# Sink attention into experts on one core: side products issued later, and the first expert's two column blocks interleaved

## The chip, the cores and the metric

One core of a Trainium2 chip. The metric is the device time of one execution of the program in microseconds (us); of three runs the median before is 1338.66 us (1338.24 to 1338.86). TensorE (PE in the profile), VectorE (DVE), ScalarE (ACT), GpSimd (POOL) and the queue on SyncE (SP) each work through their own instructions in program order.

## The reference

```python
# attention: q, k, v of 2 batches x 8 heads x 768 positions x 64
keep = (pos_k < 4) | ((pos_q - pos_k >= 0) & (pos_q - pos_k < 128))
a = softmax(where(keep, q @ k.T / 8, -1e9));  x = a @ v          # -> 1536 x 512
# mixture of 8 experts, D = 512, F = 1024
P = exp(x @ w_gate - max);  8 times: rows to 1, columns to 1, times 1536/8
out = sum_e P[:, e] * (relu(x @ w1[e]) @ w2[e])
# last layer, 512 -> 2048 -> 512
h = out @ w_in;  return (h * cos(h)) @ w_out
```

## The kernel before

All precise products are made from float16 pairs, a high part and a low part, so each matrix product is three products on TensorE. Tensors are scaled by a power of two first. `scales` (L122) finds that factor: VectorE cuts the maxima to powers of two, ScalarE writes them on the diagonals of small matrices (L139), a matmul with ones (`product`, L146) spreads them over all partitions, and VectorE reads the result back (L151). `split` (L173) makes the pair: the high part on ScalarE (or VectorE, where `by` is set), and one step later the low part, usually on VectorE (L183, or L177 without a factor).

**The order is written out by hand.** `put(t0, every, steps)` enters functions into a table of steps, and `run(n)` issues step n: first what was left in the list `late` in the step before, then what the table has for n. A function that appends to `late` thus postpones its work by one step. In the expert part the same is done by `tick`, once after each group of matmuls.

**The attention** works through 48 units (batch b, head pair p, 128 queries i), 24 for each batch. Unit k starts in step 2k (2k+4 in batch 1): `scores` on TensorE (L525) into two banks of the ring "s"; VectorE masks them and takes the maximum (L535); ScalarE exponentiates (L545) and rounds to float16 (`high`, L568) into a buffer of the ring `a16s`; GpSimd makes the low part (L574); SP issues a transposing DMA (`turn`, L584); 13 steps after its scores the unit's products with v follow (`values`, L597 and L602) and VectorE divides by the row sum (`norm`, L614). The ring `a16s` has five buffers, and three from step 58 on; the ring "s" has four banks, and two from step 58 on.

`prep_v` (L433) makes the float16 pair of v for one batch: maxima, one call of `scales` for a group of head pairs (which writes n diagonals into `W1O` and multiplies n times), then for each head pair the split (`sp`) and `sinks` (L463), two matmuls with the matrix `rep` (L466) that copy out the four sink rows, and one VectorE operation (L467). `prep_gate` does it for the gate's weights, `w_load` for an expert's.

`x_operand` (L186) makes the first expert layer's moving operand of 128 tokens from the attention's output: three sums (L197 to L199), high parts on ScalarE, low parts, and a transposing DMA on SP (L205) into `XO`. In batch 0 this happens six times, for c = 0, 1 and i = 0, 1, 2, in steps 37, 41, 45, 53, 57 and 61.

**The first expert layer** replaces a 2 x 2 block product by seven products (numbered o = 0 to 6) of prepared sums of blocks. `w1_split` (L251) makes the sums of the weights on GpSimd (L266 to L269) and their pairs in `W1O`, for one of four column blocks j in four steps. In `g1` (L923) two column blocks, c = 0 and 1, belong to one call, and `chain` names the order of the 14 products (L960, six matmuls each). Products 0, 4, 3 and 6 of a block add up in one bank ("A"), 5 and 2 in another ("B"), 1 has a third ("C"); after 0, 4 and 3 ScalarE copies the sum so far out of "A" (L928), and VectorE adds pairs (L932). `ONE` is the chain of the first expert's first batch, in which the "B" bank of both blocks is the same bank:

```python
ONE = tuple((c, o) for c in range(2) for o in (0, 5, 4, 1, 3, 6, 2))
banks(A0=(2,), A1=(7,), B0=(3,), B1=(3,), C=(6,), g2=(5, 7), l=(5,))
```

Steps up to 69 are issued before the experts. From step 70 on the attention's steps are spread over the ticks of the first expert's first batch: one step per product for 27 ticks, then two steps in three ticks. `g2_mm` (L1028) is the second layer. The weights of the first expert's second layer come through two buffers that they share with the sums of `w1_split`.

Of the kernel before, what the change touches and what calls it, by code (L numbers as in the profile page):

```python
# [40 lines left out]
def kernel(  # L41
# [14 lines left out]
    nc = tc.nc  # L56
# [65 lines left out]
    def scales(parts, n, clamp, keep, tag, then, squares=False, out=None):  # L122
# [34 lines left out]
        late.append(lambda: late.append(product))  # L157
# [8 lines left out]
    late = []  # L166

# [44 lines left out]
    wsc = {}  # L212
# [9 lines left out]
    def w_load(e, nm, place, st, junk=None):  # L222
# [21 lines left out]
        def scl():  # L244
            m = sm.tile([128, 1], F32, tag="wmm", name="wmm")
            nc.vector.tensor_reduce(out=m, in_=st[nm, "m"], axis=AX.X, op=ALU.max)
            scales(m, 1, 1e-30, res, f"{nm}{e}", lambda *s: wsc.update({(e, nm): s}), junk is not None)
# [50 lines left out]
    def attention():  # L298
# [134 lines left out]
        def prep_v(b, groups):  # L433
# [13 lines left out]
            def scl(g, sq):  # L447
                scales(m[:, g], g.stop - g.start, 1e-30, sm, "", lambda *s: None, sq, (sv[:, g], siv_[:, g]))
# [25 lines left out]
            for n, g in enumerate(groups):  # L474
# [5 lines left out]
                for p in range(g.start, g.stop):  # L480
                    steps.append(lambda p=p: sp(p))
                    steps.append(lambda p=p: sinks(p))
# [4 lines left out]
        def prep_gate():  # L487
            wgm = sm.tile([128, 1], F32, tag="wgm", name="wgm")
            absmax(wgm, wgf.rearrange("p k e -> p (k e)"))

            def then(s, si):
                split(wg[:, 0], wg[:, 1], wgf, s)
                swg.append(si)

            scales(wgm, 1, 1e-30, res, "wg", then)
# [195 lines left out]
        def ops(b, c, i, s0):  # L691
            box = []
            put(s0, 1, [lambda: box.append(x_operand(
                b, c, i, None, *(() if b else ((Ts, xss), *((nc.gpsimd, nc.vector)[n] for n in ((0, 0), (1, 0))[c])))))])
            put(s0 + 2, 1, [lambda: box.pop()()])
# [26 lines left out]
        put(15, 2.5, p0[10:-1:2])  # L722
        put(26, 1, [prep_gate])
        put(12, 1.5, wl1[4:])
        put(28, 2.75, w1_split(0, st, range(1)))
        put(14, 2.0, [lambda p=p: load_v(1, p) for p in range(NP)])
        p1 = prep_v(1, (slice(0, NP),))
        put(24, 2.5, p1[-1:] + p1[:5] + [lambda: None] + p1[5:-1])

        def run(n):  # L730
            flush()
# [4 lines left out]
        for n in range(-2, start):  # L736
            if n == ends[0] - 8:

                banks(s=(0, 1), x=(4,))
                a16s.parts[3:] = []  # L740
# [4 lines left out]
                w1_split(0, st, range(1, NJ)))  # L745
# [49 lines left out]
    def experts(before):  # L795
# [124 lines left out]
        ONE = tuple((c, o) for c in range(2) for o in (0, 5, 4, 1, 3, 6, 2))  # L920
# [224 lines left out]
        put(0, 1, w1_rest[:4])  # L1145
        put(4, 1, w1_rest[4:8])
        put(9, 1, w1_rest[8:])
# [108 lines left out]
```

## Time and profile before

| | |
|---|---|
| median of three runs | 1338.66 us |
| the profiled execution: own time | 1336.99 us |
| its span, first to last instruction | 1335.2 us |
| busy: PE / DVE / ACT / POOL | 1266.1 / 837.5 / 708.1 / 653.9 us |
| TensorE's clock, mean granted share | 0.976 |

A row of a timeline gives the start (us from the span's start), the duration, engine, line, operation, output and inputs, and in brackets how long the engine had been idle before it and what ended the wait. A row of the waits gives the waiting instruction, whom it waited for, total us, how often, and the longest. L numbers are lines of the kernel.

### The profile page before, as it was taken

The numbers are of one execution on the slowest core, as the hardware profiler recorded it, in microseconds if no ns is written. First come the engines' busy times: TensorE is split into PE (matmuls) and PEld (weight loads), VectorE is DVE, ScalarE is ACT, GpSimd is POOL, SyncE is SP. The second block draws the span as 40 slices with busy tenths as digits, with TensorE's granted clock in tenths as the row PEclk, the third lists the DMA queues.
The fourth block names the chain that finished last, engine by engine and source line by source line (L and its number), as shares of the span: only waits on it lengthen the run. The fifth ranks groups of instructions, "written<-read, shape, count | busy, mean of one in ns | idle before, by whom it ended". The sixth has DMA issues, their size and how long they took to land.

```text
span 1335.2 us, 19606 instructions
## 1 busy us (share of the span) xinstructions
PE 1266.1 (95%) x7269; PEld 676.5 (51%) x7269; DVE 837.5 (63%) x1608; ACT 708.1 (53%) x1493; POOL 653.9 (49%) x817
## 2 busy tenths in 40 slices
PE   5657899999999999999999999999999998999998
PEld 4544546555554545555454555545455544445454
DVE  6676624765548555853755575375556688788674
ACT  7866836373633537163353716335372757566452
POOL 5766664340633454272335427233541857376543
PEclk7868999999999999999999999999999998999999
DMA  9988661021013210501321150132102241400001
GB/s 259 172 172 169 139 116 58 9 107 64 13 64 111 95 64 32 174 0 64 112 94 63 32 174 1 63 112 94 64 32 83 52 105 28 105 1 1 32 17 48
DMA packets 135472, 106.67 MB, mean 80 GB/s; under 512 B 98000, under 2 KB 110288, under 8 KB 135376
## 3 DMA queue, kind: packets, MB, share of 16 engines
q1 hardware_dynamic: 121296, 75.12, 21.7%
q0 software_dynamic: 7168, 25.17, 6.0%
q10 hardware_dynamic: 6912, 5.13, 1.3%
q8 instruction: 57, 0.93, 0.3%
q14 instruction: 39, 0.32, 0.1%
HBM read 70.27 MB, written 11.53 MB: 61 GB/s over the span
## 4 chain that ended last, share of the span: by engine, by line
PE 71%; DVE 5%; POOL 4%; ACT 3%; issue 3%; DMA 1%; POOLq 0%; DVEq 0%; ACTq 0%
PE bank L1028 38%; PE bank L960 28%; PE bank L977 4%; DVE tmp L991 2%; DVE tmp L897 1%; DMA xo<-xs 1%; POOL hh L877 1%; DVE tmp L888 1%; ACT xs L182 1%; DVE xs L183 1%; ACT tmp L885 0%; ACT tmp L893 0%; POOL S L268 0%; DVE w1o L183 0%; POOL S L269 0%
## 5 line engine op out<-in xcount | busy, mean ns | idle before, releaser
L1028 PE MATMUL bank<-w2s,hh 128*128 128x512 f16 x2880 | 637.0, 379 | 2.6 <-POOL hh L901 2.1
L960 PE MATMUL bank<-xo,w1o 128*128 128x384 f16 x2688 | 448.9, 327 | 11.3 <-ACT acc L928 7.4
L1028 PEld LDWEIGHTS <-hh 128*128 128x128 f16 x2880 | 281.2, 98 | 334.7 <-POOL hh L901 4.8
L877 POOL TENSOR_TENSOR hh<-tmp,hh 128x384 f16<-128x384 f32 x240 | 217.6, 927 | 352.7 <-ACT tmp L876 350.8
L960 PEld LDWEIGHTS <-w1o 128*128 128x128 f16 x2688 | 260.9, 98 | 185.9 <-issue 16.9
L928 ACT ACTIVATE tmp<-bank 128x384 f32<-128x384 f32 x180 | 87.5, 487 | 300.0 <-PE bank L960 299.9
L932 DVE TENSOR_TENSOR tmp<-bank,tmp 128x384 f32<-128x384 f32 x180 | 97.6, 554 | 175.9 <-ACT tmp L928 130.8
L977 PE MATMUL bank<-xo,w1o 128*128 128x384 f16 x672 | 120.4, 329 | 6.5 <-ACT tmp L999 3.6
L1097 DVE SCALAR_TENSOR_TENSOR acc<-bank,PS,acc 128x512 f32<-128x512 f32 x84 | 62.9, 748 | 81.6 <-PE bank L1028 81.2
L876 ACT ACTIVATE tmp<-tmp 128x384 f32<-128x384 f32 x180 | 94.2, 523 | 5.7
L977 PEld LDWEIGHTS <-w1o 128*128 128x128 f16 x672 | 66.0, 99 | 58.0 <-issue 10.9
L875 ACT ACTIVATE hh<-tmp 128x384 f16<-128x384 f32 x180 | 92.6, 515 | 1.8 <-DVE tmp L932 1.7
L899 POOL TENSOR_SCALAR hh<-tmp 128x384 f16<-128x384 f32 x64 | 45.7, 715 | 82.7 <-DVE tmp L897 72.9
L182 ACT ACTIVATE w1o<-S,s 128x1024 f16<-128x1024 f32 x40 | 45.8, 1145 | 74.4 <-POOL S L269 74.4
L160 DVE TENSOR_REDUCE wm<-st 128x1 f32<-128x1024 f32 x68 | 81.5, 1208 | 0.0
L183 DVE SCALAR_TENSOR_TENSOR w1o<-st,s,w1o 128x512 f16<-128x512 f32 x72 | 65.1, 935 | 14.0 <-ACT w1o L182 13.9
L183 DVE SCALAR_TENSOR_TENSOR w1o<-S,s,w1o 128x1024 f16<-128x1024 f32 x40 | 55.2, 1381 | 26.6 <-ACT w1o L182 26.6
L901 POOL TENSOR_TENSOR hh<-tmp,hh 128x384 f16<-128x384 f32 x64 | 68.8, 1076 | 5.3
L183 DVE SCALAR_TENSOR_TENSOR w2s<-st,s,w2s 128x512 f16<-128x512 f32 x72 | 60.2, 848 | 17.5 <-ACT w2s L182 17.4
L991 DVE TENSOR_TENSOR tmp<-bank,tmp 128x384 f32<-128x384 f32 x112 | 59.1, 548 | 10.9 <-PE bank L977 6.7
L574 POOL TENSOR_TENSOR parts<-xo,parts 128x512 f16<-128x512 f32 (+1 forms) x38 | 42.8, 1125 | 24.5 <-ACT parts L568 18.3
L893 ACT ACTIVATE tmp<-tmp,scl 128x384 f32<-128x384 f32 x64 | 39.1, 610 | 26.9 <-DVE tmp L888 26.9
(187 smaller groups left out, 1308.2 us busy)
## 6 DMA issues: line engine op xcount, KB each, us to landing
st<-in_moe_w_dram SPq DMA_DIRECT2D x56, 512.0 KB, 6.0
f<-in_moe_w_in_dram POOLq DMA_DIRECT2D x16, 512.0 KB, 4.4
f<-in_moe_w_out_dram POOLq DMA_DIRECT2D x16, 512.0 KB, 4.2
w2p<-in_moe_w_dram SPq DMA_DIRECT2D x8, 512.0 KB, 4.3
w_in<-x POOLq DMA_DIRECT2D x16, 256.0 KB, 4.4
w_out<-x POOLq DMA_DIRECT2D x16, 256.0 KB, 4.2
st<-w_out SPq DMA_DIRECT2D x8, 512.0 KB, 5.4
st<-w_in SPq DMA_DIRECT2D x8, 512.0 KB, 6.5
```

What stands on the lines that cost most here:

```text
L160: nc.vector.tensor_reduce(out=dst, in_=src, axis=axis, op=ALU.max, apply_absolute_value=True)
L183: late.append(lambda: nc.vector.scalar_tensor_tensor(out=lo, in0=src, scalar=s, in1=hi, op0=ALU.mult, op1=ALU.subtract))
L875: nc.scalar.activation(out=hi, in_=src, func=AF.Relu)
L876: nc.scalar.activation(out=dst, in_=src, func=AF.Relu)
L877: nc.gpsimd.tensor_tensor(out=lo, in0=dst, in1=hi, op=ALU.subtract)
L901: nc.gpsimd.tensor_tensor(out=lo, in0=k, in1=hi, op=ALU.subtract)
L928: nc.scalar.activation(out=t, in_=ps, func=AF.Copy)
L932: nc.vector.tensor_tensor(out=t, in0=ps, in1=t, op=ALU.add)
L960: nc.tensor.matmul(ps, W1O[:, j0 + c, wi, o, kk, :], XO[b][:, kk, o, xi, :], start=(n == 0 and o in (0, 5, 1)), stop=(n == 5), skip_group_ ...
L977: nc.tensor.matmul(ps, W1O[:, j, wi, o, kk, :], XO[b][:, kk, o, xi, :], start=(n == 0), stop=(n == 5))
L991: nc.vector.tensor_tensor(out=t, in0=x, in1=y, op=ALU.add)
L1028: nc.tensor.matmul(ps, HH[:, hi, f, t * 128:(t + 1) * 128], w[:, wi, f, :], start=(f == order[0] and n == 0), stop=(f == order[-1] and n = ...
```

## The change

- `scales` gets the argument `lag`, the number of steps from the diagonals to the matmul: 2 as before, 3 for the second group of batch 0, 5 for the group of batch 1, the gate and the first expert's first weights. `later(n, f)` puts f off by n steps.
- The sink rows of batch 0 (head pairs 1 to 3) move from steps 15, 17 and 20 to 19, 24 and 29; those of batch 1 are issued six steps after their place in the list. The list of batch 1 is spaced by two steps, not two and a half, with two empty entries more.
- The last operand block of batch 0 (c = 1, i = 2) makes the pair of its sums one step sooner, with the low part on VectorE, not GpSimd; its DMA follows one step sooner.
- The sums and pairs of column block j = 1 are made in steps 58 to 62, not in ticks 0 to 4; those of j = 2 and 3 in ticks 2 to 5 and 7 to 10, not 4 to 7 and 9 to 12.
- The ring `a16s` keeps five buffers up to step 77.
- `ONE` alternates between the blocks c = 0 and c = 1.

```diff
--- before.py
+++ after.py
@@ -119,7 +119,7 @@
     diag = res.tile([128, 128], BF16, name="diag")
     top_bank = ["l"]
-    def scales(parts, n, clamp, keep, tag, then, squares=False, out=None):
+    def scales(parts, n, clamp, keep, tag, then, squares=False, out=None, lag=2):
@@ -154,7 +154,7 @@
             then(s, si)
-        late.append(lambda: late.append(product))
+        later(lag, product)
     def absmax(dst, src, axis=AX.X):
         nc.vector.tensor_reduce(out=dst, in_=src, axis=axis, op=ALU.max, apply_absolute_value=True)
@@ -164,6 +164,9 @@
     BW = ((1, 1, 0), (0, 1, 0), (1, 0, 0), (0, 1, 0))
     late = []
+
+    def later(n, f):
+        late.append(f if n <= 1 else lambda: later(n - 1, f))
     def flush():
         now, late[:] = late[:], []
@@ -244,7 +247,8 @@
         def scl():
             m = sm.tile([128, 1], F32, tag="wmm", name="wmm")
             nc.vector.tensor_reduce(out=m, in_=st[nm, "m"], axis=AX.X, op=ALU.max)
-            scales(m, 1, 1e-30, res, f"{nm}{e}", lambda *s: wsc.update({(e, nm): s}), junk is not None)
+            scales(m, 1, 1e-30, res, f"{nm}{e}", lambda *s: wsc.update({(e, nm): s}), junk is not None,
+                   lag=5 if e == 0 else 2)
         return [lambda i=i: load(i) for i in range(4)] + [lambda i=i: amax(i) for i in range(4)] + [scl]
@@ -445,7 +449,8 @@
                     absmax(m[:, p:p + 1], vt[:, p].rearrange("p t c -> p (t c)"))
             def scl(g, sq):
-                scales(m[:, g], g.stop - g.start, 1e-30, sm, "", lambda *s: None, sq, (sv[:, g], siv_[:, g]))
+                scales(m[:, g], g.stop - g.start, 1e-30, sm, "", lambda *s: None, sq, (sv[:, g], siv_[:, g]),
+                       5 if b else 3 if g.start else 2)
             def common():
@@ -479,7 +484,7 @@
                     steps.append(common)
                 for p in range(g.start, g.stop):
                     steps.append(lambda p=p: sp(p))
-                    steps.append(lambda p=p: sinks(p))
+                    steps.append(lambda p=p: later(6, lambda: sinks(p)) if b else sinks(p))
             return steps + [ones_col]
         swg = []
@@ -492,7 +497,7 @@
                 split(wg[:, 0], wg[:, 1], wgf, s)
                 swg.append(si)
-            scales(wgm, 1, 1e-30, res, "wg", then)
+            scales(wgm, 1, 1e-30, res, "wg", then, lag=5)
@@ -690,9 +695,11 @@
         def ops(b, c, i, s0):
             box = []
+            last = not b and c and i == U3 - 1
             put(s0, 1, [lambda: box.append(x_operand(
-                b, c, i, None, *(() if b else ((Ts, xss), *((nc.gpsimd, nc.vector)[n] for n in ((0, 0), (1, 0))[c])))))])
-            put(s0 + 2, 1, [lambda: box.pop()()])
+                b, c, i, None, *(() if b else (
+                    (Ts, xss), *((nc.gpsimd, nc.vector)[n] for n in ((0, 0), (1, int(last)))[c])))))])
+            put(s0 + (1 if last else 2), 1, [lambda: box.pop()()])
         ends = []
         for b in range(B):
@@ -719,15 +726,18 @@
         put(6, 1.0, p0[4:7])
         put(9, 4, p0[7:9])
         put(13, 0.5, p0[9:-1:2])
-        put(15, 2.5, p0[10:-1:2])
+        put(19, 5, p0[10:-1:2])
         put(26, 1, [prep_gate])
         put(12, 1.5, wl1[4:])
         put(28, 2.75, w1_split(0, st, range(1)))
+        put(ends[0] - 8, 1.25, w1_split(0, st, range(1, 2)))
         put(14, 2.0, [lambda p=p: load_v(1, p) for p in range(NP)])
         p1 = prep_v(1, (slice(0, NP),))
-        put(24, 2.5, p1[-1:] + p1[:5] + [lambda: None] + p1[5:-1])
+        put(24, 2.0, p1[-1:] + p1[:5] + [lambda: None] * 3 + p1[5:-1])
         def run(n):
+            if n == start + 8:
+                a16s.parts[3:] = []
             flush()
             for f in at.pop(n, ()):
                 f()
@@ -737,12 +747,11 @@
             if n == ends[0] - 8:
                 banks(s=(0, 1), x=(4,))
-                a16s.parts[3:] = []
             run(n)
         gates = [[lambda b=b, i=i: gate(b, i) for i in range(NT)] for b in range(B)]
         return ([lambda n=n: run(n) for n in range(start, ends[1])], gates, probabilities,
-                w1_split(0, st, range(1, NJ)))
+                w1_split(0, st, range(2, NJ)))
     def sinkhorn():
@@ -917,7 +926,8 @@
         CHAIN = ((0, 0), (1, 0), (0, 5), (0, 4), (1, 4), (1, 5), (0, 3), (1, 3), (0, 1), (0, 6), (1, 6),
                  (0, 2), (1, 2), (1, 1))
-        ONE = tuple((c, o) for c in range(2) for o in (0, 5, 4, 1, 3, 6, 2))
+        ONE = ((0, 0), (0, 5), (1, 0), (0, 4), (0, 1), (0, 3), (1, 4), (0, 2), (0, 6), (1, 5), (1, 3), (1, 1),
+               (1, 6), (1, 2))
         HOME = {0: "A", 4: "A", 3: "A", 6: "A", 5: "B", 2: "B", 1: "C"}
         def g1(b, j0, chain, act):
@@ -1142,9 +1152,8 @@
             put(1, 1, [f()])
         put(5, 4, [lambda f=f: gate(f) for f in gates[0]])
-        put(0, 1, w1_rest[:4])
-        put(4, 1, w1_rest[4:8])
-        put(9, 1, w1_rest[8:])
+        put(2, 1, w1_rest[:4])
+        put(7, 1, w1_rest[4:])
         a = ACC[0].rearrange("p t c -> p (t c)")
         ring["c"] = Ring(a[:, n * HT:(n + 1) * HT] for n in range(8))
         put(T0 + 0, 2, [lambda f=f: gate(f) for f in gates[1]])
```

## Rows read from the trace of the kernel before

**Rows 1.** Six stretches: us, length, busy us (instructions) by engine, granted clock, DMA.

```profile
0.00:62.00 62.00, 38.37 (x301) 29.14 (x302) 41.16 (x154) 47.62 (x135) 39.22 (x89) 0.83 1.00 221
62.00:100.00 38.00, 22.30 (x187) 15.18 (x187) 26.55 (x91) 23.88 (x68) 24.92 (x33) 0.66 0.88 169
100.00:140.00 40.00, 29.79 (x270) 17.13 (x267) 27.29 (x67) 26.88 (x66) 26.30 (x32) 0.90 0.75 156
140.00:164.20 24.20, 21.63 (x245) 13.16 (x244) 14.55 (x47) 22.48 (x57) 15.72 (x20) 1.00 0.70 156
164.20:178.70 14.50, 12.05 (x123) 6.61 (x120) 6.46 (x19) 8.05 (x21) 10.40 (x17) 1.00 0.53 101
178.70:1335.20 1156.50, 1141.92 (x6163) 595.28 (x6158) 721.47 (x1233) 579.17 (x1149) 537.37 (x629) 1.00 0.21 65
```

**Rows 2.** Waits of PE, 0 to 62 us: total us, times, longest.

```profile
PE bank L146 <- ACT w1o L139: 6.8, 2, 3.5
...
PE bank L597 <- DVE hh L467: 3.0, 2, 2.6
PE bank L146 <- ACT diag L139: 2.4, 2, 2.3
```

**Rows 3.** Waits of ACT, 9 to 62 us.

```profile
ACT nm L538 <- DVE mx L535: 4.0, 4, 1.5
```

**Rows 4.** Waits of PE, 62 to 100 us.

```profile
PE bank L525 <- DVE mx L535: 4.6, 4, 1.9
...
PE bank L466 <- DVE w2s L183: 3.4, 3, 1.6
PE bank L466 <- ACT w2s L182: 2.4, 3, 1.3
```

**Rows 5.** One stretch; columns: PE, PEld, DVE, ACT, POOL, clock, DMA.

```profile
74.90:86.70 11.80, 8.52 (x75) 5.70 (x75) 10.39 (x37) 5.75 (x18) 4.97 (x8) 0.61 0.88 191
```

**Rows 6.** Same stretch, tile w1o (PE, PEld, DVE, ACT), then S (DVE, ACT, POOL).

```profile
106.50:114.70 8.20, 3.42 (x18) 1.60 (x18) 4.09 (x4) 1.84 (x2) 1.00 0.55 120
...
106.50:114.70 8.20, 1.27 (x1) 1.14 (x1) 3.29 (x4) 1.00 0.55 120
```

**Rows 7.** Timeline of DVE, low parts of two operand blocks.

```profile
85.41 0.62 DVE L177 TENSOR_TENSOR w2s<-acc,w2s 128x256 f16<-128x256 f32 x2
...
92.27 1.57 DVE L177 TENSOR_TENSOR w2s<-acc,w2s 128x256 f16<-128x256 f32 x2
```

**Rows 8.** Timeline of POOL at 92 to 97 us.

```profile
92.36 1.33 POOL L574 TENSOR_TENSOR parts<-xo,parts 128x512 f16<-128x512 f32 x1 [1.52 <-ACT parts L568]
...
95.37 1.16 POOL L177 TENSOR_TENSOR w2s<-hh,w2s 128x512 f16<-128x512 f32 x1 [1.47 <-ACT w2s L176]
```

**Rows 9.** Timeline of SP's queue at 96 to 105 us.

```profile
96.56 2.11 SPq L205 DMA_TRANSPOSE xo<-w2s  x1
98.77 5.76 SPq L584 DMA_TRANSPOSE parts<-parts  x3
```

**Rows 10.** Timeline of ACT at 98 to 104 us.

```profile
103.78 0.42 ACT L568 ACTIVATE parts<-xo 128x256 f16<-128x256 f32 x1 [5.25 <-DMA parts<-parts]
```

**Rows 11.** Timeline of PE, three places in the first expert.

```profile
102.83 0.65 PE L960 MATMUL bank<-xo,w1o 128*128 128x384 f16 x3 [1.68 <-DMA xo<-w2s]
...
116.00 2.08 PE L960 MATMUL bank<-xo,w1o 128*128 128x384 f16 x6 [3.85 <-ACT acc L928]
...
123.20 1.15 PE L960 MATMUL bank<-xo,w1o 128*128 128x384 f16 x6
```

**Rows 12.** One stretch of 3 us, all engines.

```profile
116.00:119.00 3.00, 3.00 (x19) 1.46 (x19) 2.90 (x7) 2.39 (x7) 2.92 (x5) 0.50 0.91 192
```

**Rows 13.** Waits of PE, 100 to 164 us.

```profile
PE bank L960 <- ACT acc L928: 7.4, 6, 3.9
...
PE bank L960 <- DVE acc L932: 1.6, 1, 1.6
PE bank L146 <- ACT diag L139: 1.2, 1, 1.2
```

## The prediction

> **What bounds the kernel now.** I read the busy time by stage first, then each engine's waits in the stages where TensorE is not full, then the timelines around the longest waits. From 178.7 us on TensorE is busy for 1141.92 of 1156.5 us [rows 1]; nothing of the change is issued there, so all of its effect lies in the first 178.7 us. Those are four stages. From 0 to 62 us (the attention's first batch) ScalarE is the fullest engine, 47.62 of 62 us. From 62 to 100 us (the second batch up to the first expert) no engine is full on average. From 100 to 164.2 us the first expert's first layer and the second batch share all engines: TensorE is idle for 40.0 - 29.79 = 10.2 us in the first 40 and for 24.2 - 21.63 = 2.6 us in the rest, where ScalarE works for 22.48 of 24.2 us, 93%. The last 14.5 us are nearly all TensorE [rows 1].
>
> **The change part by part.** The profiled execution took 1336.99 us for a span of 1335.2, so 1.8 us lie around the span, and it stands 1.7 us under the median of 1338.66. I work out the difference on the span and apply it to the median.
>
> *Later products, 0 to 62 us.* TensorE stood 6.8 us before the matmuls of the two grouped `scales` calls, 2.4 us before those of single ones, and 3.0 us before values products held up by the sink rows' VectorE operation [rows 2]. One of the two grouped waits stays: for batch 0 the lag goes from two steps to three, from step 11 to step 12, ahead of the scores of that step, and TensorE is given nothing between the two, so its place in the queue is the same. The others go. But TensorE is not what this stage waits for. ScalarE does the same work as before, and of its waits only those for VectorE's maxima, 4.0 us in all [rows 3], can be later scores in disguise. That is the ceiling; the floor is nothing (the maxima are late because of VectorE's own queue, which holds the low parts of v). I see late scores behind about half: gain **2.0** (0 to 4.0).
>
> *Sink rows of batch 1, and the work that moves in, 62 to 102.8 us.* TensorE's waits before the sink products are 3.4 + 2.4 = 5.8 us [rows 4]. They vanish when the products come six steps later, behind the splits that they read. Most of that was hidden: VectorE is busy for 10.39 of 11.8 us between 74.9 and 86.7 us [rows 5], and the scores after it wait for VectorE to free banks (4.6 us [rows 4]). I count 0.7 us as a gain, for the one place where the first scores of batch 1 stood behind sink products. Against it, four steps for block j = 1 move into steps 58 to 62. Their price is in the trace, where they now run: 4.09 us on VectorE in four operations, 1.84 us on ScalarE in two, and 3.29 us on GpSimd in four [rows 6]. The last operand block's low part also goes to VectorE. A 512-wide one does not occur there in the rows; two shorter ones took 0.62 us at 85.41 and 1.57 us at 92.27 [rows 7]. I take the lower, as the GpSimd operation that ran beside the slow pair [rows 8] need not be there, and keep 1.57 for the range. So VectorE gets 4.7 us more, in front of scores that have two banks only. Some falls into VectorE's own idle time: 38.0 - 26.55 = 11.5 us in the stage [rows 1], of which half lies after step 58. Three quarters of the 4.7 hidden leaves 1.2 us. GpSimd's 3.29 us come in front of low parts that SP's transposes wait for; GpSimd is idle for 38.0 - 24.92 = 13.1 us, so I cost it at 0.5, and at 3.3 if that cover is gone.
>
> The operand comes sooner: SP began the last operand's DMA at 96.56 us, when GpSimd's 1.16 us at 95.37 were done, and spent 2.11 us on it; three transposes stood behind it until 104.5 [rows 8, 9]; the first product went on at 102.83 after waiting 1.68 us for that DMA [rows 11]. One step sooner, it goes ahead of one more transpose, and a low part late on VectorE would hold that one up. The sooner step undoes part of the shift. Sum for this stage: +1.2 + 0.5 - 0.7 = a loss of **1.0** (a gain of 2 if all is hidden and the 1.7 us wait goes; a loss of 4.7 if nothing of VectorE's work is hidden).
>
> In a sentence of its own: the Trainium skill ("SBUF — State Buffer", section "SBUF: two separate sides") says that GpSimd and a VectorE operation with two SBUF inputs exclude each other on a shared port, one standing still until the other is done, which speaks against putting GpSimd's sums and VectorE's low parts into the same steps. The pairs of 0.62 and 1.57 us agree with it; by the rule each of the three low parts of j = 1 could take 0.95 us more, and this stage would lose 3.9, not 1.0.
>
> *Buffers kept longer, and the first expert, 100 to 164.2 us.* ScalarE stood for 5.25 us up to 103.78 because its next `high` needed a buffer that the queued transposes still read [rows 10]. Two more buffers let it run on; the copy that the third product waits for then comes in time. TensorE's waits here are 7.4 us for ScalarE's copies out of bank "A" (six times), 1.6 for VectorE on the shared bank "B", and 1.2 for the diagonal of the second weights [rows 13], which keeps its lag of two. The new chain leaves one to three products of the other block between a product in "A" and the next in that bank; in the old one product 6 followed 3 at once. So I let the 7.4 go. The "B" pairs have one product between them as before, and the shared bank is handed over as often: 0.8 of 1.6 goes. Of the rest of TensorE's 12.8 us of idle time, 1.7 is the DMA counted above and I take nothing.
>
> There is a second gain. After 3.85 us idle the six matmuls at 116.00 took 2.08 us, where six take 1.15 at 123.20 [rows 11]; the granted clock from 116 to 119 was 0.50 [rows 12], the lower of the two levels, 1.2 GHz. Without the wait that product is 0.9 us shorter. The Trainium skill ("TensorE: Matmul & The Clock Gate", Part 1) has the throttled state as what idling returns the array to; the row agrees.
>
> Together 7.4 + 0.8 + 0.9 = 9.1 us. Part comes back. From 140 us ScalarE is 93% busy and nothing is taken off it there, so at most 1.7 us of that stretch can go, and elsewhere ScalarE and VectorE must now do the same copies and sums in less time. Block j = 1 no longer costs 1.84 us on ScalarE and 4.09 on VectorE here, which helps. I take three quarters: gain **7.0** (2, if each removed wait is replaced by the "B" wait; 11.1, if all idle time but the DMA's goes). The transfers of the second weights are spaced in ticks and have shorter ticks; their buffers change hands with the sums for j = 2 and 3, which move by the same two ticks; I cost that at nothing, and at 1.5 us, one tick at the stage's pace, if a transfer comes late.
>
> *164.2 us to the end.* The same instructions in the same order: 0 (-1 to +1).
>
> Sum: -2.0 + 1.0 - 7.0 = -8.0 us. Span 1327.2, own time 1329.0, median **1330.7**.
>
> **The rivals.**
> *TensorE becomes the bound.* All its idle time in the first expert goes but the 1.2 for the diagonal and the 1.7 for the DMA: 12.8 - 2.9 = 9.9, with 0.9 for the clock 10.8; the first stage gives 3.0 and the second loses nothing: -13.8, 1324.9. For it: each of the three other engines works under 69% of 100 to 140 us [rows 1]. Against: all are in order, and each product's result passes ScalarE, VectorE, ScalarE and GpSimd.
> *The waits were cover.* ScalarE and VectorE set the pace everywhere; TensorE waits elsewhere instead. First stage 0, second +1.5, third -2.5 (clock and half of the longest wait): -1.0, 1337.7. For it: ScalarE's 77% in the first stage and 93% at the end. Against: 5.25 us of ScalarE's idle time [rows 10] is bought off by buffers, not by order.
> *The moved split delays the start.* The low parts of j = 1 stand in VectorE's queue ahead of the maxima, each waiting for ScalarE's high part, while scores have two banks. The 4.7 us are bare, and two waits like the one before the last sink low part (longest 1.6 [rows 4]) add 3.2: +7.9 by the first product, which starts near 109 us; the first expert gives back 5: +2.9, 1341.6. It decides from a first product later than about 107.
>
> **How the numbers follow.** The forecast (1326 to 1336) has 0.54, TensorE as the bound 0.18, waits as cover 0.17, the delayed start 0.11. 0.2% is 2.7 us and about what a measurement can tell from no change; so faster means under 1336.0: 0.54 + 0.18 = 0.72. Same is the third case, 0.17, and slower 0.11. The range goes from 1323.5, which leaves out the further half of the second case, to 1340, which leaves out most of the last. The bounds of the terms sum to 1320.5 (-4.0 - 2.0 - 11.1 - 1.0) and 1342.4 (0 + 4.7 - 2.0 + 1.0).
>
> **What would show it.** TensorE's waits for diagonals and sink splits should be gone but for one of about 3 us near 18 us. ScalarE should have no wait of several us before L568. The first product should start between 100 and 104 us, and TensorE's idle time from there to the second layer should be near 5 us, not 12.8, with the granted clock at 1 throughout. The second layer should begin near 158 us instead of 164.2. I am wrong if the first product starts after 107, or if the wait for L928 reappears as a wait for L932 of like size.

## The result: slower by 0.67%, all of it before the first expert's first product

The median went from 1338.22 us (six runs of the kernel before beside it) to 1346.94 us; the ratio is 1.0067, with a 95% interval of 1.0057 to 1.0077, so about 9 us were lost. Forecast were 1330.7 us, with 1323.5 to 1340.0 as the range. The profiled execution after took 1346.12 us for a span of 1344.4, 9.2 us above the span before.

Six stretches of the changed kernel, in the columns of [rows 1] (us, length, busy us of PE, PEld, DVE, ACT, POOL, clock, DMA). The second one now ends with the first product, the fourth with the second layer:

```profile
0.00:62.00 62.00, 38.12 (x302) 28.83 (x303) 40.64 (x150) 47.37 (x133) 38.28 (x89) 0.86 0.99 221
62.00:112.70 50.70, 23.11 (x186) 15.54 (x185) 34.57 (x99) 28.33 (x79) 30.09 (x39) 0.55 0.82 146
112.70:152.70 40.00, 34.88 (x325) 20.27 (x323) 28.06 (x75) 28.79 (x74) 26.14 (x34) 0.88 0.76 162
152.70:172.30 19.60, 17.64 (x195) 10.74 (x192) 11.77 (x37) 15.76 (x39) 9.61 (x13) 1.00 0.55 131
172.30:188.20 15.90, 12.21 (x124) 6.69 (x121) 6.14 (x17) 9.33 (x25) 11.79 (x18) 1.00 0.49 94
188.20:1344.40 1156.20, 1140.86 (x6158) 594.71 (x6156) 721.76 (x1233) 579.15 (x1149) 537.52 (x629) 1.00 0.21 65
```

The second one before, up to where the first product went on:

```profile
62.00:102.80 40.80, 23.44 (x189) 15.46 (x189) 27.52 (x94) 23.88 (x68) 24.92 (x33) 0.67 0.91 176
```

The last stretch takes 1156.2 us as against 1156.5. The loss is the second: TensorE is busy for 23.11 us in it, much as before, but takes 50.7 us over that and not 40.8, at a mean clock of 0.55. VectorE's busy time rose from 27.52 to 34.57 us.

TensorE's waits, 0 to 62 us, to set beside [rows 2]:

```profile
PE bank L530 <- DVE mx L540: 7.7, 5, 3.3
...
PE bank L146 <- ACT w1o L139: 3.2, 1, 3.2
```

The waits for diagonals and sink rows are gone but for one of 3.2 us (and 0.4 us for a sink split), as forecast. In their place stand 7.7 us before the scores (L530; L525 before) for VectorE's maxima. The first scores of batch 1 begin at 75.92 us, not 76.21. Whether the stage gave anything at all can't be told from that: of kernels whose steps are the same up to there, `before` has 76.21, `buffers_only` 77.21 and `split_alone` 78.96 in their one profile each. All later stretches are therefore counted from these scores.

TensorE's waits from the first product to the second layer, to set beside [rows 13]:

```profile
PE bank L970 <- DVE acc L942: 2.8, 3, 1.0
PE bank L530 <- DVE mx L540: 2.4, 2, 2.2
PE bank L970 <- ACT acc L938: 1.1, 2, 0.9
```

The waits for ScalarE's copies, 7.4 us before, became 1.1, as the interleaved chain should bring. But the stretch shrank only from 61.4 to 59.6 us.

Three places in TensorE's timeline (start, duration, engine, line, operation, xcount, idle time before):

```profile
111.87 0.40 PE L602 MATMUL bank<-w2s,parts 128*128 128x130 f16 x2 [5.80 <-DMA parts<-parts]
...
112.74 2.11 PE L970 MATMUL bank<-xo,w1o 128*128 128x384 f16 x6
...
178.11 0.34 PE L607 MATMUL bank<-w2s,parts 128*128 128x65 f16 x6 [3.01 <-DVE acc L619]
```

The first product, 99.99 us before (and again after its DMA at 102.83 [rows 11]), starts at 112.74. It is not its own operand that is late (sent at 100.76 us, landed at 105.3): ahead of it in TensorE's queue stands a values product that waited 5.80 us for a transposing DMA. The first product runs at the lower clock, 2.11 us for six matmuls where 1.15 is the time at the higher one [rows 11]. The 0.9 us that I had thought to save at 116.00 [rows 11] did not come: over the whole first layer the mean granted clock is 0.92, where it was 0.94 before.

### The profile page after: what moved, and what is told of

Its sections match the earlier page's. It is cut to its first block, busy times and chain, and to the rows that moved or that the text cites. A ratio compares the mean times of both kernels' runs of the same rounds, so it can differ in the third digit from the quotient of the medians.

```text
span 1344.4 us, 19614 instructions
## 1 busy us (share of the span) xinstructions
PE 1266.8 (94%) x7269; PEld 676.8 (50%) x7269; DVE 843.0 (63%) x1609; ACT 708.7 (53%) x1493; POOL 653.4 (49%) x816
## 4 chain that ended last, share of the span: by engine, by line
PE 70%; DVE 5%; POOL 4%; ACT 3%; issue 3%; DMA 1%; POOLq 0%; DVEq 0%; ACTq 0%
PE bank L1038 38%; PE bank L970 28%; PE bank L987 4%; DVE tmp L1001 2%; DVE tmp L906 1%; DMA xo<-xs 1%; POOL hh L886 1%; DVE tmp L897 1%; ACT xs L185 1%; DVE xs L186 0%; ACT tmp L894 0%; ACT tmp L902 0%; POOL S L272 0%; POOL S L273 0%; POOL hh L910 0%
## 5 line engine op out<-in xcount | busy, mean ns | idle before, releaser
L987 PEld LDWEIGHTS <-w1o 128*128 128x128 f16 x672 | 65.9, 98 | 57.6 <-issue 10.2
L186 DVE SCALAR_TENSOR_TENSOR w1o<-st,s,w1o 128x512 f16<-128x512 f32 x72 | 64.7, 930 | 14.0 <-ACT w1o L185 13.9
L186 DVE SCALAR_TENSOR_TENSOR w2s<-st,s,w2s 128x512 f16<-128x512 f32 x72 | 60.2, 848 | 17.5 <-ACT w2s L185 17.4
L186 DVE SCALAR_TENSOR_TENSOR w1o<-S,s,w1o 128x1024 f16<-128x1024 f32 x40 | 54.6, 1365 | 23.2 <-ACT w1o L185 23.2
L579 POOL TENSOR_TENSOR parts<-xo,parts 128x512 f16<-128x512 f32 (+1 forms) x34 | 38.9, 1145 | 31.2 <-ACT parts L573 16.8
```

Of the source, the lines that this page charges most:

```text
L186: late.append(lambda: nc.vector.scalar_tensor_tensor(out=lo, in0=src, scalar=s, in1=hi, op0=ALU.mult, op1=ALU.subtract))
L987: nc.tensor.matmul(ps, W1O[:, j, wi, o, kk, :], XO[b][:, kk, o, xi, :], start=(n == 0), stop=(n == 5))
```

## The experiments

In short, three parts of the change delay the first product. The later products put a split of v in front of the first maxima (2.6 us, won back elsewhere). The moved split fills VectorE's queue, and its sums on GpSimd lengthen VectorE's other operations (3.9 us). The sooner operand holds up a transpose, which then lands late (4.2 us). What the interleaved chain wins in waits it loses again.

All ratios are to the kernel before, run beside it on the same chip; the difference of two ratios is uncertain by about 0.14%, or 1.9 us. Times of stretches come from one profile each: **M** from the first scores of batch 1 to VectorE's first maximum of them; **Q** from there to the first product (to its restart, where it waits for its operand's DMA); **F** from there to the second layer; **T** from there to the end of the last values products. Between kernels that differ elsewhere only, M agrees within 0.4 us (3.6 to 4.0), T within 0.1, Q and F within about 1. Where the first product has a restart, about half of its six matmuls lie before it and count to Q; the changed kernel, `split_undone` and `last_sooner_gpsimd` have none. The letters of the theories in the expectations have nothing to do with the letters of the stretches.

| kernel | ratio, 95% interval | M | Q | F | T |
|---|---|---|---|---|---|
| before | 1 | 1.25 | 25.4 | 61.4 | 14.6 |
| after | 1.0067 (1.0057 to 1.0077) | 3.9 | 33.0 | 59.6 | 15.9 |
| last_undone | 1.0038 (1.0024 to 1.0052) | 3.7 | 28.7 | 59.9 | 17.0 |
| split_undone | 1.0026 (1.0017 to 1.0036) | 3.8 | 26.9 | 62.5 | 14.6 |
| both_undone | 0.9989 (0.9980 to 0.9999) | 3.8 | 24.8 | 59.8 | 14.6 |
| last_sooner_gpsimd | 1.0003 (0.9993 to 1.0013) | 3.6 | 25.6 | 61.0 | 14.6 |
| last_on_vector | 0.9984 (0.9975 to 0.9994) | 4.0 | 24.1 | 58.9 | 14.6 |
| best_again (the same kernel) | 0.9994 (0.9985 to 1.0003) | 3.7 | 24.0 | 59.3 | 14.6 |
| split_alone | 1.0025 (1.0016 to 1.0034) | 1.25 | 29.2 | 59.0 | 17.0 |
| early_split_new_chain | 1.0036 (1.0025 to 1.0048) | 8.1 | 24.1 | 58.8 | 17.0 |
| early_split_old_chain | 1.0020 (1.0011 to 1.0030) | 8.1 | 24.3 | 58.3 | 14.6 |
| sums_on_vector | 1.0025 (1.0016 to 1.0035) | 8.4 | 24.6 | 60.1 | 14.6 |
| vector_load | 1.0001 (0.9990 to 1.0011) | 3.7 | 26.2 | 58.9 | 14.6 |
| gpsimd_load | 1.0014 (1.0005 to 1.0024) | 3.8 | 27.1 | 58.9 | 14.6 |
| lags_only | 1.0008 (0.9997 to 1.0019) | 3.8 | 26.3 | 59.9 | 14.6 |
| buffers_only | 0.9992 (0.9982 to 1.0001) | 1.25 | 26.4 | 58.9 | 14.6 |
| w2_vector_old | 0.9999 (0.9990 to 1.0009) | 4.0 | 24.3 | 60.8 | 14.7 |
| w2_vector_new | 1.0019 (1.0010 to 1.0028) | 8.2 | 24.7 | 59.7 | 14.6 |

### Undoing the two suspects

`last_undone` takes back the operand block, `split_undone` the moved split and the chain, `both_undone` both, so that the later products and the five buffers stay. `split_alone` has nothing but the split and the chain on top of the kernel before.

```diff
# last_undone
-            last = not b and c and i == U3 - 1
+            last = False
# split_undone
-        put(ends[0] - 8, 1.25, w1_split(0, st, range(1, 2)))
-                w1_split(0, st, range(2, NJ)))
+                w1_split(0, st, range(1, NJ)))
-        put(2, 1, w1_rest[:4])
-        put(7, 1, w1_rest[4:])
+        put(0, 1, w1_rest[:4])
+        put(4, 1, w1_rest[4:8])
+        put(9, 1, w1_rest[8:])
-        ONE = ((0, 0), (0, 5), (1, 0), ...)
+        ONE = tuple((c, o) for c in range(2) for o in (0, 5, 4, 1, 3, 6, 2))
```

> The changed kernel with the last operand block as before: low part of its sums on GpSimd, one step later. Theory Q (SP's queue: the DMA of the last operand, now ahead of more transposes and waiting for a low part late on VectorE, holds up the transposes behind it, and TensorE waits 5.8 us for them at 111.87): most of the loss comes back, time 1339 to 1341, first product of the first expert near 106 us, no wait over 2 us before values products there. Theory V (VectorE: the low parts of block j = 1 in steps 58 to 62 stand ahead of the maxima, scores with two banks come 6.9 us later): only the 1.6 us of that low part come back, 1344 to 1346, first product at 110 or later.

> The changed kernel with the old order of the chain ONE and with the sums and pairs of blocks j = 1, 2, 3 in ticks 0, 4 and 9 as before; the last operand block stays sooner and on VectorE. Theory V: the maxima come in time, first product near 102 us, and the first expert loses its interleaving, 1336 to 1339. Theory Q: the DMA of the last operand still stands ahead of the transposes, so TensorE still waits 3 to 6 us before values products near step 67, 1341 to 1345.

> The changed kernel with the last operand block, the chain ONE and the times of the splits as before; later products, later sink rows and five buffers stay. Both theories: the loss is gone. If the later products are worth the 2.0 us that I gave them and the buffers take away the wait of ScalarE at 103.78 (5.25 us): 1331 to 1336. If these waits were cover only: 1337 to 1339.

> The kernel before with the interleaved chain ONE and the block j = 1 made in steps 58 to 62, nothing else. Theory V: the maxima of steps 59 to 65 come 5 to 7 us later and the interleaved chain gives back 2 to 5, so 1340 to 1345. Theory Q: without the sooner operand the queue on SP is not held up, so 1334 to 1339.

Measured: 1.0038, 1.0026, 0.9989 and, for `split_alone`, 1.0025. With both undone the loss is gone. Each theory was half right: the time of `last_undone` (1344.47 us) is what V expects, that of `split_undone` (1342.68 us) what Q expects. From `both_undone`, split and chain cost 0.49% (6.6 us), the operand block 0.37% (5.0 us); together they cost 0.78%, a little less than the sum. The table says where. From `both_undone` to `last_undone` Q grows by 3.9 us, and T by 2.4; from there to the changed kernel Q grows by another 4.2. With M, where the later products add 2.6 and Q gives back 0.5, that is 2.6 - 0.5 + 3.9 + 4.2 = 10.2 us, all of the added time between the first scores of batch 1 and the first product. `split_alone` agrees: without the later products M is 1.25, and Q is 3.8 above the kernel before.

### The operand block: which half of the edit

`last_sooner_gpsimd` makes it one step sooner with the low part still on GpSimd, `last_on_vector` puts the low part on VectorE in the old step; both have split and chain undone, as `both_undone` has. The lines are against `split_undone`:

```diff
# last_sooner_gpsimd
-   (nc.gpsimd, nc.vector)[n] for n in ((0, 0), (1, int(last)))[c]
+   (nc.gpsimd, nc.vector)[n] for n in ((0, 0), (1, 0))[c]
# last_on_vector
-            put(s0 + (1 if last else 2), 1, [lambda: box.pop()()])
+            put(s0 + 2, 1, [lambda: box.pop()()])
```

> As both_undone (1337.9), but the last operand block one step sooner, its low part still on GpSimd. Theory Q: its DMA now stands ahead of one more transpose that is ready, and waits for a low part made no sooner than before: values products wait 4 to 6 us, 1341 to 1344. If it were only the work on VectorE: 1337 to 1339.

> As both_undone (1337.9), but the last operand block's low part on VectorE, in its old step. Theory Q: the order on SP is the old one, so no more than the 0.7 to 1.6 us of that operation, 1337 to 1340. If VectorE's load is the cause of the 4.8 us between split_undone and both_undone: 1341 to 1343.

Measured 1.0003 and 0.9984: the sooner step costs about 0.14%, which is as much as the uncertainty and less than theory Q expected (1340.07 us, not 1341 to 1344), though its values product waited as Q had it, for 5.73 us. VectorE alone costs nothing. The low part of 128x512 took 1.64 us on VectorE in the changed kernel (timeline below), a little over my upper bound of 1.57. Both halves in one cost 0.37%. SP's queue shows how. First `both_undone`, then `split_undone`, which differ by this edit alone (L208 is the operand's DMA, L589 the transposes):

```profile
93.07 3.27 SPq L589 DMA_TRANSPOSE parts<-parts  x2
97.70 3.44 SPq L208 DMA_TRANSPOSE xo<-w2s  x1
```

```profile
95.03 1.81 SPq L589 DMA_TRANSPOSE parts<-parts  x1
97.57 1.51 SPq L208 DMA_TRANSPOSE xo<-w2s  x1
99.18 5.45 SPq L589 DMA_TRANSPOSE parts<-parts  x2
```

TensorE in `split_undone`:

```profile
108.31 0.40 PE L602 MATMUL bank<-w2s,parts 128*128 128x130 f16 x2 [5.43 <-DMA parts<-parts]
```

The operand's DMA has overtaken one transpose. Counted from VectorE's first maximum (80.35 and 82.32 us) it leaves 2.1 us sooner, and the second transpose of the pair at 93.07 now goes behind it, first in the issue at 99.18. In `both_undone` the values product ahead of the first product starts at 100.26 without a wait for a transpose; in `split_undone` it waits 5.43 us. What was gained for the operand is lost on the product ahead of it in TensorE's queue. That is 2.0 us in Q and, as only `both_undone` has a restart, part of the 2.7 in F.

The later issue alone does not make that wait. The DMA view of the issue gives the time from issue to landing (the last number, in us); the transpose in `both_undone`, and then in `split_undone`, where the loads of k and q for the next head pair are under way with it:

```profile
parts<-parts SPq DMA_TRANSPOSE x1, 3.3
```

```profile
xo<-in_k_dram ACTq DMA_DIRECT2D x1, 384.0 KB, 5.1
xo<-in_q_dram ACTq DMA_DIRECT2D x1, 384.0 KB, 8.2
parts<-parts SPq DMA_TRANSPOSE x1, 9.1
```

Sent at 99.18 and landed after 3.3 us, it would have been there at 102.5, before TensorE stood idle at 102.9. It is the 9.1 us that TensorE waits for. In all 18 profiles the first transposing DMA that SP sends from 0.6 us before the k load on takes 6.0 to 9.5 us to land, those that it sends from 88 us up to then 2.9 to 4.6. With the old block that first one is the operand's DMA; in the changed kernel and in `split_undone` it is the transpose for which the values product ahead of the first product waits. In `last_sooner_gpsimd` both were hit, 7.8 us for the operand and 8.0 for the transpose right behind it.

### The moved split: place, and the chain by itself

`early_split_new_chain` makes the sums and pairs of j = 1 twelve steps sooner (46 to 50), before the first scores of batch 1, with the last block undone; `early_split_old_chain` has the old `ONE` besides.

```diff
-        put(ends[0] - 8, 1.25, w1_split(0, st, range(1, 2)))
+        put(46, 1.25, w1_split(0, st, range(1, 2)))
```

> The changed kernel with the last operand block as before and the sums and pairs of block j = 1 in steps 46 to 50, where no scores are issued, not 58 to 62. Theory V: the maxima of steps 59 to 65 no longer stand behind them, first product near 104 us, 1335 to 1339. If the loss of last_undone (1344.5) comes from the interleaved chain or from the total work, not its place: 1342 to 1345.

> As early_split_new_chain with the old chain ONE. My forecast had the new chain worth about 6 us of TensorE's waits, so this would be 1340 to 1345. If ScalarE sets the pace from step 70 to the end of the attention and TensorE's waits were its cover, the two chains differ by less than 2 us.

Measured 1.0036 and 1.0020. The place hardly matters (1.0036 against 1.0038; theory V had the loss gone), so the idea that the split costs only because of where it stands falls. The split costs some 0.31% (from 0.9989 to 1.0020), and the chain is no gain but a loss of 0.16%, just over the uncertainty. TensorE's waits from the first product to the second layer, new chain and then old:

```profile
PE bank L970 <- DVE acc L942: 2.8, 3, 1.0
PE bank L530 <- DVE mx L540: 2.5, 2, 2.2
...
PE bank L970 <- ACT acc L938: 0.6, 2, 0.4
```

```profile
PE bank L969 <- ACT acc L937: 6.2, 5, 2.9
...
PE bank L969 <- DVE acc L941: 1.1, 1, 1.1
PE bank L530 <- DVE mx L540: 0.8, 1, 0.8
```

And the whole stretch, new and then old (columns as in [rows 1]):

```profile
108.07:166.90 58.83, 52.32 (x507) 31.14 (x507) 37.62 (x108) 43.95 (x110) 34.76 (x45) 0.91 0.71 158
```

```profile
110.76:169.07 58.31, 50.20 (x507) 30.20 (x507) 36.33 (x106) 45.05 (x113) 36.40 (x46) 0.94 0.71 160
```

Of 6.2 us of waits for ScalarE 5.6 went; 3.4 came back as waits for VectorE (1.7 each for its sums and its maxima), and the same 507 matmuls took 2.1 us longer, at a mean clock of 0.91 instead of 0.94. The clock is from one profile each. What paces the first layer then is not shown: ScalarE is busy for 75 and 77% of it.

### Is it VectorE's queue or GpSimd's?

From `both_undone`: `vector_load` adds four reductions of 128x1024 (1.21 us each) to VectorE in steps 59 to 62, `gpsimd_load` makes the four sums of j = 1 once more on GpSimd in step 58. Their results are used by nobody, or are the same.

```diff
# vector_load
+        waste = sm.tile([128, 4], F32, tag="waste", name="waste")
+        put(59, 1, [lambda n=n: absmax(waste[:, n:n + 1], st["w1"][:, n, 0:1024]) for n in range(4)])
# gpsimd_load
+        put(58, 1, w1_split(0, st, range(1, 2))[:1])
# sums_on_vector (early_split_old_chain and this)
-                g = nc.gpsimd
+                g = nc.vector if e == 0 and j == 1 else nc.gpsimd
```

> As both_undone (ratio 0.9989, about 1338), with four more VectorE reductions of 1024 elements (1.2 us each, 4.8 in all, result unused) in steps 59 to 62, nothing else. Theory W (VectorE's work is the path of the second batch, so what is added there is added to the first product): 4 to 5 us, 1342 to 1343. If the split's loss came by ScalarE or GpSimd, or by the waits between engines: 0 to 2 us.

> As both_undone, with the four GpSimd sums of block j = 1 (3.3 us) made once more in step 58, their result unused. Theory W: 0 to 1.5 us, what they hold up on the shared port and in front of the transposes, 1337 to 1339.5. If GpSimd's low parts ahead of the transposes are the path: 2 to 4 us, 1340 to 1342.

> early_split_old_chain with one change: the four sums of block j = 1 are made on VectorE instead of GpSimd. Before kernel about 1339; early_split_old_chain was 1342.6 (ratio 1.0020). Theory G (the moved split costs by GpSimd's 3.3 us of sums, which also hold up VectorE's two-input operations): 2 to 3.5 us come back, ratio 0.9995 to 1.0005, 1338.5 to 1340, first scores of batch 1 to the first product's restart about 30 us instead of 32.3. Theory V (it costs by VectorE's queue, which now gets some 1.7 us more): the same or slower, ratio 1.0020 to 1.0035, 1342 to 1344.

Measured 1.0001, 1.0014 and 1.0025: against 0.9989, VectorE's 4.8 us cost 0.12% (1.6 us), within the uncertainty, and GpSimd's 3.3 us of sums 0.25% (3.3 us, give or take 1.9). Both speak against theory W, which had 4 to 5 us for the first and at most 1.5 for the second. Taking the sums off GpSimd, though, bought nothing: theory G, that GpSimd's sums carry the split's price, fails as I had put it. The windows join the two. Here is the stretch in which VectorE makes the maxima of the first seven units of batch 1, for `both_undone`, `gpsimd_load`, `vector_load`, `last_undone` and the changed kernel, one after the other (the third busy time is VectorE's):

```profile
80.35:96.86 16.51, 10.77 (x74) 6.95 (x74) 14.82 (x54) 11.40 (x33) 7.75 (x10) 0.50 0.75 141
```

```profile
80.97:99.51 18.54, 11.19 (x74) 7.29 (x74) 17.19 (x54) 11.32 (x33) 11.55 (x14) 0.50 0.66 127
```

```profile
81.02:100.21 19.19, 10.13 (x74) 6.61 (x74) 17.84 (x58) 11.42 (x33) 7.39 (x10) 0.59 0.70 133
```

```profile
82.31:103.58 21.27, 11.19 (x74) 7.29 (x74) 18.49 (x58) 13.06 (x36) 12.22 (x14) 0.50 0.61 116
```

```profile
79.79:102.61 22.82, 11.19 (x74) 7.28 (x74) 19.86 (x59) 13.58 (x38) 12.66 (x14) 0.50 0.56 107
```

VectorE is busy for 87 to 93% in all of them, more than any other engine: it is the bound here. GpSimd's sums bring no instruction to it (54 in both), yet add 2.4 us to its busy time. Its timeline in the changed kernel and GpSimd's beside it show how:

```profile
87.74 0.70 DVE L202 TENSOR_TENSOR hh<-acc,hh 128x128 f32<-128x128 f32 x1
88.36 2.10 DVE L180 TENSOR_TENSOR w2s<-acc,w2s 128x256 f16<-128x256 f32 x2
...
92.56 1.13 DVE L186 SCALAR_TENSOR_TENSOR w1o<-tmp,s,w1o 128x512 f16<-128x512 f32 x1 [1.06 <-ACT w1o L185]
...
96.77 0.29 DVE L202 TENSOR_TENSOR hh<-acc,hh 128x128 f32<-128x128 f32 x1
96.97 0.62 DVE L180 TENSOR_TENSOR w2s<-acc,w2s 128x256 f16<-128x256 f32 x2
...
97.88 1.28 DVE L186 SCALAR_TENSOR_TENSOR w1o<-S,s,w1o 128x1024 f16<-128x1024 f32 x1 [0.29 <-ACT w1o L185]
99.09 1.64 DVE L180 TENSOR_TENSOR w2s<-hh,w2s 128x512 f16<-128x512 f32 x1
```

```profile
85.08 1.44 POOL L270 TENSOR_TENSOR S<-tmp 128x256 f32<-128x256 f32 x1
...
87.52 0.78 POOL L272 TENSOR_TENSOR S<-tmp 128x256 f32<-128x256 f32 x1
88.25 0.77 POOL L273 TENSOR_TENSOR S<-tmp,S 128x256 f32<-128x256 f32 x1
88.99 1.33 POOL L579 TENSOR_TENSOR parts<-xo,parts 128x512 f16<-128x512 f32 x1
```

Beside the last sum and the low part that follows it on GpSimd, VectorE's pair L180 takes 2.10 us, later 0.62; L202 takes 0.70 beside the third sum, later 0.29. So of the 4.8 us by which this stretch is longer in `last_undone` than in `both_undone`, the sums make 2.0 (`gpsimd_load`) through VectorE; the other 2.8 is what remains bare, that is hidden by nothing, of VectorE's own four operations of the split (3.3 us, two shown above) and of its waits of 1.06 and 0.29 us for ScalarE's high parts. The same clash seems to work the other way in `vector_load`: its reductions put two operations, which take 1.10 and 1.58 us beside GpSimd's in `both_undone`, at places where they take 0.42 and 1.00, and the stretch grows by 2.7 for 4.8. In `early_split_old_chain` both stand before the first maxima, as M shows (8.1 us, not 3.8); with the sums on VectorE M is 8.4. The low parts there, first with the sums on GpSimd, then on VectorE:

```profile
77.54 1.59 DVE L186 SCALAR_TENSOR_TENSOR w1o<-tmp,s,w1o 128x512 f16<-128x512 f32 x1 [1.40 <-ACT w1o L185]
...
80.49 1.25 DVE L186 SCALAR_TENSOR_TENSOR w1o<-tmp,s,w1o 128x256 f16<-128x256 f32 x1
```

```profile
77.28 1.14 DVE L186 SCALAR_TENSOR_TENSOR w1o<-tmp,s,w1o 128x512 f16<-128x512 f32 x1 [1.40 <-ACT w1o L185]
...
79.67 0.48 DVE L186 SCALAR_TENSOR_TENSOR w1o<-tmp,s,w1o 128x256 f16<-128x256 f32 x1
```

The two low parts get 1.2 us shorter, and the four sums take 2.5 us of VectorE, before these: nothing is left over. VectorE pays either way.

### ScalarE's backlog in the tail

With the interleaved chain T grew from 14.6 to 15.9 or 17.0 us; I had put that stretch at 0 (within 1). The last wait is 3.01 us now (178.11 above), where it was 1.77 us. Where T is 17.0, the mean granted clock of that stretch is 0.90, where it is 15.9 or 14.6 it is 1.00: the rest of the loss is TensorE at the lower clock. `w2_vector_old` and `w2_vector_new` make the high parts of the first expert's second weights on VectorE, on top of `last_on_vector` and of `early_split_new_chain`.

```diff
-  split(W2S[0][:, 0, f], W2S[0][:, 1, f], box.pop(n), wsc[0, "w2"][0])
+  split(W2S[0][:, 0, f], W2S[0][:, 1, f], box.pop(n), wsc[0, "w2"][0], by=1)
```

> As last_on_vector (ratio 0.9984), the high parts of the first expert's second weights (four of 1.14 us on ScalarE) made on VectorE. Theory T (ScalarE sets the pace from the first product to the end of the attention): 1 to 4 us faster, 1333 to 1336.5. If TensorE or VectorE set it: the same or slower, 1337 to 1340.

> As early_split_new_chain (ratio 1.0036) with the same four high parts on VectorE. Theory T: the new chain's wait of 3 us ahead of the last values products, which stands for ScalarE's backlog, goes: 3 to 5 us faster, 1339 to 1341. If the chain itself costs the time (its shared bank): under 2 us faster, 1342 to 1345.

Measured 0.9999 and 1.0019. On the new chain T falls to 14.6 and the ratio from 1.0036 to 1.0019, 2.3 us and so between the two expectations; TensorE's last wait becomes

```profile
173.45 0.34 PE L607 MATMUL bank<-w2s,parts 128*128 128x65 f16 x6 [1.74 <-DVE acc L619]
```

So what the chain costs at the end is ScalarE's backlog: its last high part of the weights comes later, and VectorE's division stands behind the low part. On the old chain the same edit gains nothing (0.9999, where the kernel without it had 0.9984 and then 0.9994), which speaks against ScalarE as what paces the first layer there.

### What the rest of the change is worth

`lags_only` has just the later products and sink rows, `buffers_only` just the five buffers up to step 77; `best_again` is `last_on_vector` measured a second time.

```diff
# buffers_only, in the kernel before
         def run(n):
+            if n == start + 8:
+                a16s.parts[3:] = []
...
-                a16s.parts[3:] = []
```

> The changed kernel with only the later products for scales and sink rows left (last operand, split, chain and buffers as before). both_undone, which also keeps five buffers, was 0.9989. If the later products carry that gain: ratio 0.9985 to 0.9993, 1337 to 1338. If the buffers carry it: 0.9995 to 1.0005, 1338.5 to 1339.7, with ScalarE's wait of some 5 us for a buffer still there.

> The kernel before with five buffers of a16s up to step 77 and nothing else. If the buffers carry the 0.11% of both_undone: ratio 0.9985 to 0.9993 (1337 to 1338) and no wait of ScalarE for a buffer. If the later products carry it: 0.9996 to 1.0004, the 5 us of ScalarE's wait turning into a wait elsewhere.

> last_on_vector once more, with more rounds: later products, five buffers, and the low part of the last operand block on VectorE in its old step. The first time: ratio 0.9984 [0.9975, 0.9994]. If it beats the kernel before, ratio 0.9980 to 0.9992 (about 1337.5) and the interval stays under 1; if that was chance, 0.9995 to 1.0005 with 1 inside.

Measured 1.0008, 0.9992 and 0.9994 (0.9985 to 1.0003). The later products alone give nothing; M is 3.8 us in `lags_only` and 1.25 in `buffers_only`, since with the new list VectorE has a split of v in front of the first maxima (L183 and L186, 0.67 and 1.02 us in the changed kernel; the same two stood behind them before). ScalarE's wait for a buffer, `lags_only` and then the changed kernel:

```profile
ACT parts L573 <- DMA parts<-parts: 8.2, 2, 7.3
```

```profile
111.90 0.63 ACT L573 ACTIVATE parts<-xo 128x512 f16<-128x512 f32 x1 [4.92 <-DMA parts<-parts]
```

In the changed kernel the wait ends with the same transpose that the values product waited for. `buffers_only` has no such wait, and F is 58.9 us instead of 61.4; its 0.08% is not clear of no change. That `last_on_vector` beats the kernel before (0.9984 the first time) is not confirmed by the second time, whose interval holds 1.

## Why the prediction was wrong

**The stage that I put at a loss of 1.0 lost about 10.** First scores of batch 1 to first product: 26.6 us before, 36.8 after (+10.2). Four steps of that sum failed.

*VectorE's new work and its cover.* I took VectorE's idle time as a mean over 38 us and hid three quarters of 4.7 us in it. The row that forbids this was already used in the same part for another edit: 10.39 of 11.8 us busy [rows 5]. I had 1.2 us; 2.8 us were bare. `vector_load` with 1.6 us for 4.8 seems to agree with me, but it got there by moving other operations to where they were shorter and by giving back 1.3 of 2.7 before the first product; VectorE's idle time in the stretch fell only from 1.7 to 1.4 us.

*GpSimd's sums.* Costed at 0.5, 3.3 at worst; `gpsimd_load` measured 3.3 (give or take 1.9), of which its profile shows 2.0 in the stretch of the maxima. The idle time of GpSimd was no cover, since the price is paid by VectorE. Here the sentence of the Trainium skill that I had weighed ("SBUF — State Buffer", "SBUF: two separate sides") was nearer than my sum. By it the stage would have lost 2.9 us more than I had; the trace agrees with 2.4 us of busy time on VectorE for no instruction more, though most of it fell on the operands' sums and low parts (L201, L202, L180), not on the low parts of j = 1 that I had named. Those took 3.3 us in all, less than the 4.09 of [rows 6].

*The operand's DMA.* I wrote that it goes ahead of one more transpose and that a low part late on VectorE would hold that one up, and gave it no price. It was 4.2 us in Q. The low part ended at 100.73 us in the changed kernel, and SP, which had sent the transpose before at 94.80, began the DMA at 100.76 and the next transposes at 102.37:

```profile
100.76 1.51 SPq L208 DMA_TRANSPOSE xo<-w2s  x1
102.37 5.96 SPq L589 DMA_TRANSPOSE parts<-parts  x2
```

The first of these two landed 9.4 us after its issue; in `last_undone` the same transpose took 3.5. That a transpose which is held up would then run beside the loads of k and q, and take that much longer to land, was not in the prediction at all.

*The later products.* I had 0.7 us as their gain in this stage. M grew by 2.6 us instead, in `lags_only` as in the changed kernel, as VectorE's split of v now stands in front of the first maxima. What the later products and the buffers gave back in Q and F left the sum of the two at 0.9989.

**The first expert's 7.0 us measured 0.5.** F and T together went from 76.0 to 75.5. The mechanism (a copy out of "A" no longer waited for) was right, the worth of it was not: "three quarters" of the waits was too much, as products then waited for VectorE and ran at the lower clock. What F did gain, 1.8 us, `both_undone` nearly has with the old chain (1.6), that is with the buffers; between the two early splits the new chain's F is 0.5 us the longer. ScalarE's wait for a buffer, which the prediction had gone, is still 4.92 us in the changed kernel. The 0 for the tail missed 1.2.

**The first stage's 2.0 is not to be seen**: the 0.3 us of the profile are less than profiles of the same steps differ by. ScalarE still waits 3.8 us for VectorE's maxima (4.0 in [rows 3]), so the scores had hardly been what it waited for; that the gain is nothing, the lower end of my bound, fits.

**The rivals.** The delayed start came true (first product at 112.74, beyond its 107), but only in part by its mechanism, VectorE's queue ahead of the maxima: split and sums together are 3.9 of the 10.2 us, where it had 7.9, and the operand's DMA and the later products, which it did not have, are the rest. It had 5 given back by the first expert, and 0.5 were. So its total, a loss, is nearer by luck than its terms are. "The waits were cover" fits the first stage and most of the first expert. I had put 0.11 on the delayed start and let the sum of the edits' gains decide.

## What to carry to other kernels

Before work is moved into a stretch, look at the window in which the receiving engine feeds the next stage, not at its mean idle time; and ask what that engine's neighbours take from it, since an engine with time to spare can still lengthen another's instructions. In an in-order queue a transfer issued sooner is a transfer put in front of another: name that other one, who waits for it, and what else will be in transfer by the time it is sent. A wait that is removed in front of the bound engine only counts once something else than the next in-order wait is named to follow it.

## What the runs showed of the hardware that was not expected

Beside GpSimd's operations VectorE's operations with two inputs took up to 3.4 times as long (2.10 us against 0.62), and the first of the sums on GpSimd itself 1.44 us against 0.73; the four reductions with one input in `vector_load` took 1.21 us each, beside GpSimd's operations or not. Transposing DMAs sent from 0.6 us before the k load on took 6.0 to 9.5 us to land for the first of them, in all 18 profiles, where those before took 2.9 to 4.6. That the loads of k and q make them slow is argued from this timing; no run moved the loads by themselves.
